# One rotation of four PSUM pairs after the tail, conversions one step a block, and the last stage's rows gathered four blocks ahead of their mixing

## The chip, the cores and the metric

The kernel runs on one core of a Trainium2 chip. The metric is device time in microseconds (us), from start to end of one execution of the program. The engines named below are PE (TensorE, matrix products), DVE (VectorE), ACT (ScalarE), POOL (GpSimd) and SP (SyncE, which here only issues DMAs). Each works through its own list of instructions in order and waits on semaphores for the others.

## The reference

Three layers follow each other on 2304 tokens of width 512, all in float32:

```
scores = q @ k.T / 8                              # 4 x 8 heads, 576 x 576
attn   = softmax(scores where >= rowmax - tau)    # the others are masked
x      = attn @ v                                 # 2304 x 512

y      = logits of x @ w_gate, plus noise * log1p(exp(x @ w_noise))
for e in 8 experts:                               # each token goes to its top 2
    out[mask] += weight * (relu(x[mask] @ w1[e]) @ w2[e])

a, b   = out @ m_w1, out @ m_w2                   # 512 -> 1024 each
h      = (a * b) @ w3
result = h @ w_out                                # 1024 -> 512
```

The weights of the last layer reach the chip as float64 bit patterns; the kernel turns them into float32 itself ("conversion"). Since w3 and w_out are applied one behind the other, the kernel multiplies them once into one matrix.

## The kernel before, in words

The order of the instructions on each engine is the order in which the Python code issues them; nothing reorders it. Up to about 397 us (attention, routing, and the "tail", a hand-written list of steps that starts expert 0) the change moves nothing but the names of PSUM pools.

**Experts (397 to 899 us of the trace).** Each expert has 640 token slots in five row blocks. *Phase 1* makes the hidden layer in eight blocks f = 0 to 7 (`phase1_steps`, L767): 12 passes over 256 and 384 columns into a tile S of two PSUM banks. ACT takes the high half hh out of S (L778), DVE the low half hl (L780). S has two buffers, so block f may start when DVE is through with block f-2. *Phase 2* has five blocks j (`phase2_steps`, L799 to L801): 24 products of 512 columns into a tile o of one bank, which is scaled into y and stored to the DRAM array ydr. Beside that run, for the next expert: `x_gather` (POOL, an indirect DMA, L685) and, two blocks later, the sum of squares on ACT (`x_sq`, L694); the scaling (L700); the transposes into a tile t of one bank, with two buffers (`x_trans`, PE L714, then ACT xth L717 and DVE xtl L718); weight loads (SP), their largest square (L730), a scale per weight matrix (`w_scale`, with a product on PE in `col_all`, L151) and the split of each weight chunk into two halves (`w_split`, ACT L749, DVE L750).

**Conversions.** `conv_step` advances every live conversion by one of five stages and starts a new one every second time. Stage 0 is a load (SP), stage 2 one POOL instruction (cr, L1018) and three of DVE (L1019 to L1021), stage 3 two of POOL (L1026, L1029) around one of DVE (L1027), stage 4 a store (SP) and for the last 16 of the 40 a maximum on DVE (L1035). From expert 1 on, conv_step runs 4 times in phase 1 (f = 0, 5, 6, 7) and 9 times in phase 2 (once for j = 0, twice for j = 1 to 4); f = 1 to 4 are those in which w_split runs.

**Last stage (from 855 us).** First w3 @ w_out in eight products (`w_prod`); the first is cut in two halves around a branch that handles overflowing experts and is not taken here. Then the 18 row blocks of 128 tokens in six groups of three. For a group g, `ab(g, f)`, f = 0 to 7, makes eight blocks of a * b (PE L1339 into S, ACT, DVE, ACT, and POOL for the remainder cl); at f = 2, `outp` multiplies the group before (L1359 to L1361 into o, three times). For the next group, `y_gather` fetches each token's two expert rows from ydr (POOL, L1297), `y_mix` weighs and adds them (ACT L1304, DVE L1305, ACT L1306, three short ones on DVE, POOL L1308), `y_trans` transposes them (PE L1319). In a group, gather, mix and transpose of its row block j stand at f = j, j + 1 and j + 4 of the group before: the mix is issued one block behind its gather. While group 0 runs, the splits of the weights (`wab_split`, four; `wf_split`, six of eight) also stand in its blocks.

**PSUM.** Eight banks of 2 KB per partition. From the tail's end on: S has two buffers of two banks, t two of one, o two of one.

Of the kernel before, what the change touches and what calls it, by code (L numbers as in the profile page):

```python
# [9 lines left out]
F32 = mybir.dt.float32  # L10
F32R = mybir.dt.float32r
F16 = mybir.dt.float16
# [7 lines left out]
PSUM = bass.MemoryType.PSUM  # L20
DRAM = bass.MemoryType.DRAM

B, H, S, D = 4, 8, 576, 64
HP = H // 2
NT = B * S // 128
# [42 lines left out]
def moe_kernel(ctx, tc, qT, kT, v, tau, wgn, noise, w1, w2, m1, m2, w3T, wo, out):  # L68
# [7 lines left out]
    px = ExitStack()  # L76
    px_pool = px.enter_context(tc.tile_pool(name="px", bufs=1, space=PSUM))
    late = {}

    def ps_s():  # L80
        return psum.tile([128, 2, 512], F32, name="S")

    def ps_t():
        return psum.tile([128, 512], F32, name="t", tag="ot")

    def ps_o():
        if late:
            return late["o"].tile([128, 512], F32, name="o")
        return psum.tile([128, 512], F32, name="o", tag="ot")
# [839 lines left out]
    late["o"] = ctx.enter_context(tc.tile_pool(name="po", bufs=2, space=PSUM))  # L929
# [60 lines left out]
    SP.dma_start(table, IDX)  # L990
    cctx = ExitStack()
# [102 lines left out]
    for e in range(E):  # L1094
        more = e + 1 < E
        for f in range(8):
            if e > 0:
                if f == 1:
                    next(sc2)
                    y_scale(e, 0, NBLK)  # L1100
                if 1 <= f < 5:
                    w_split(e, 2, f - 1)
            phase1(e, f, (1,) if e == 0 else (0, 1))
            if e > 0 and f == 0:
                next(sc2)
            if more:
                if f < NBLK:
                    x_gather(e + 1, f)
                if f < 4:
                    w_load(e + 1, 1, f)  # L1110
                if 2 <= f < 2 + NBLK:
                    x_sq(e + 1, f - 2)
                if f >= 4:
                    w_sq(e + 1, 1, f - 4)
                if f == 7:
                    x_pow2(0, NBLK)
            elif f == 5:
                WOT[0] = raw_load(wA, wod[0].rearrange("p a n -> p (a n)"))
            if e > 0 and not 1 <= f < 5:
                conv_step()  # L1120
# [16 lines left out]
        for j in js:  # L1137
# [22 lines left out]
            if more:  # L1160
                if at == 0:
                    for c in range(4 if e == 0 else 2):
                        w_load(e + 1, 2, c)
                if at == 1:
                    if e > 0:
                        next(sc1)
                        for i in range(3, NBLK):
                            x_scale(e + 1, i)
                        for c in range(2, 4):
                            w_load(e + 1, 2, c)  # L1170
                if j >= 3:
                    for c in range(2):
                        w_sq(e + 1, 2, 2 * (j - 3) + c)
                if j == NBLK - 1:
                    sc2 = w_scale(e + 1, 2)
                    next(sc2)
                for _ in range(2 if e > 0 and j else 1):
                    conv_step()
# [6 lines left out]
    def w_prod(m, k0=0, k1=8):  # L1185
# [12 lines left out]
        t = wf_.tile([128, DM], F32, name="wf")  # L1198
# [17 lines left out]
    def wf_split(m):  # L1216
        t = WF[m]
        h, l = (hp_.tile([128, CAP], F16, name=n)[:, :DM] for n in ("hh", "hl"))
# [16 lines left out]
    w_prod(0, 0, 4)  # L1235
# [58 lines left out]
    def y_gather(i):  # L1294
        t = xe.tile([128, 2, DM], F32, name=("xth", "xtl")[i % 2])
# [73 lines left out]
    NGR = NT // GN  # L1369
    for m in range(8):  # L1370
# [10 lines left out]
        w_prod(m, 0 if m else 4)  # L1381
# [11 lines left out]
    for g in range(NGR):  # L1393
        for f in range(8):
# [4 lines left out]
            if g + 1 < NGR:  # L1399
                i = (g + 1) * GN  # L1400
                if 1 <= f < 1 + GN:
                    y_mix(i + f - 1)
                if f < GN:
                    y_gather(i + f)
# [8 lines left out]
            if g + 1 < NGR:  # L1413
                if 4 <= f < 4 + GN:
                    y_trans(i + f - 4)
# [44 lines left out]
```

## Time and profile before

| | |
|---|---|
| time, median of 3 runs | 1212.92 us (1211.73 to 1216.4) |
| profiled execution | 1211.47 us, of which the span from first to last instruction is 1209.1 us |
| PE busy | 1072.8 us (89% of the span) |
| DVE, ACT, POOL busy | 687.1 (57%), 632.5 (52%), 605.1 us (50%) |
| DMA | 179.62 MB, mean 149 GB/s |
| mean granted clock of PE | 0.973 |

A share of busy time is a mean over stages that differ. The chain that ended last runs through PE for most of the last stage. A row of the views below gives times in us; "x" is a count; "<-" stands between a result and its inputs, or between a waiting instruction and what released it. The granted clock is 1.00 at 2.4 GHz and 0.50 at 1.2 GHz; a value between them is a mean over a stretch.

### The profile page before, as it was taken

What the parts mean: (1) busy time and instruction counts of PE and PEld (TensorE: products, weight loads), DVE (VectorE), ACT (ScalarE), POOL (GpSimd) and SP (SyncE); (2) the same over time, 40 slices, a digit from 0 to 9 for tenths busy, and PEclk for the clock granted to TensorE, in tenths of its full rate; (3) what the DMA queues carried; (4) which work ended last, traced back from release to release, by engine and by line L of the source; (5) the groups of instructions that cost most, each with busy time, mean ns of one, the idle gap of its engine ahead of it and who ended that gap; (6) DMA issues with size and microseconds to landing.
All of it is one profiled execution on the core that took longest, in us unless ns stands there. A gap on an engine that the chain in (4) does not pass through costs nothing. (4 is left out here: it accounts for less than half of the span.)

```text
span 1209.1 us, 19702 instructions
## 1 busy us (share of the span) xinstructions
PE 1072.8 (89%) x7424; PEld 704.8 (58%) x7425; DVE 687.1 (57%) x1398; ACT 632.5 (52%) x1213; POOL 605.1 (50%) x585
## 2 busy tenths in 40 slices
PE   6888888776789799998989898989997999999998
PEld 4667666555578664645555555555774455555654
DVE  6887777788674277676676767574354321222211
ACT  6888889775543574654646464553244332322311
POOL 5888888775532056656575748450204322323211
PEclk9999999998889999999999998999998999999999
DMA  6999999966723456577775756533621112111000
GB/s 165 210 211 217 214 212 229 208 153 135 144 88 107 129 196 207 200 260 263 226 244 177 232 173 211 165 115 114 225 90 53 46 34 62 36 61 53 27 27 26
DMA packets 236193, 179.62 MB, mean 149 GB/s; under 512 B 169792, under 2 KB 192576, under 8 KB 236096
## 3 DMA queue, kind: packets, MB, share of 16 engines
q1 hardware_dynamic: 229856, 158.12, 49.7%
q0 software_dynamic: 6080, 19.93, 5.3%
q8 instruction: 59, 0.97, 0.3%
q10 hardware_dynamic: 160, 0.30, 0.1%
q14 instruction: 38, 0.31, 0.1%
HBM read 99.72 MB, written 37.30 MB: 113 GB/s over the span
## 5 line engine op out<-in xcount | busy, mean ns | idle before, releaser
L260 PE MATMUL S<-K,Q 128*128 128x288 f32 x576 | 181.8, 441 | 46.7 <-DVE p L282 41.7
L767 PE MATMUL S<-xth,w 128*128 128x256 f16 (+3 forms) x1024 | 197.2, 307 | 21.7 <-DVE hl L780 19.7
L1339 PE MATMUL S<-x2h,w 128*128 128x384 f16 x768 | 192.9, 329 | 11.0 <-DVE a__10489 L1343 7.2
L308 POOL TENSOR_TENSOR p<-p,p 128x512 f16<-128x512 f32 x140 | 159.1, 1163 | 53.0 <-ACT p L299 52.9
L767 PEld LDWEIGHTS <-w 128*128 128x128 f16 x1344 | 133.5, 99 | 83.1 <-issue 32.2
L1339 PEld LDWEIGHTS <-w 128*128 128x128 f16 x1152 | 113.5, 99 | 87.8 <-issue 16.0
L260 PEld LDWEIGHTS S<-K,Q 128*128 128x128 f32 x576 | 103.0, 199 | 74.4 <-issue 23.6
L282 DVE SCALAR_TENSOR_TENSOR p<-S,th,p 128x576 f32<-128x576 f32 x144 | 116.6, 810 | 47.9 <-ACT th L274 47.8
L271 ACT ACTIVATE p<-S,mn 128x576 f32<-128x576 f32 x144 | 105.8, 734 | 58.8 <-DVE mn L265 53.9
L1339 PE MATMUL S<-x2l,w 128*128 128x384 f16 x384 | 126.3, 329 | 0.5 <-DVE x2l L1323 0.5
L799 PE MATMUL o<-w,hh 128*128 128x512 f16 (+1 forms) x320 | 124.5, 389 | 1.0 <-ACT hh L778 1.0
L801 PE MATMUL o<-w,hl 128*128 128x512 f16 (+1 forms) x320 | 123.8, 387 | 0.0
L767 PE MATMUL S<-xtl,w 128*128 128x256 f16 (+3 forms) x512 | 121.0, 307 | 3.1 <-DVE xtl L718 3.0
L800 PE MATMUL o<-w,hh 128*128 128x512 f16 (+1 forms) x320 | 123.6, 386 | 0.0
L265 DVE TENSOR_REDUCE mn<-S 128x1 f32<-128x576 f32 x144 | 108.4, 752 | 16.6 <-PE S L260 16.2
L1018 POOL TENSOR_SCALAR cr<-s 128x512 uint32<-128x512 uint32 x40 | 82.5, 2064 | 65.7 <-DMA s<-in_wo 52.1
L749 ACT ACTIVATE w<-w,WS 128x1024 f16<-128x1024 f32 x56 | 63.2, 1143 | 58.9 <-DVE WS L139 58.9
L1029 POOL TENSOR_TENSOR ck<-ck,ct 128x512 f32<-128x512 f32 x40 | 53.4, 1334 | 77.7 <-DVE ct L1027 59.5
L780 DVE SCALAR_TENSOR_TENSOR hl<-S,hh 128x256 f16<-128x256 f32 (+3 forms) x128 | 57.3, 485 | 61.3 <-ACT hh L778 60.9
L339 PE MATMUL o<-vh,pT 128*128 128x64 f16 (+1 forms) x720 | 85.0, 199 | 5.0 <-DMA pT<-p 3.3
L750 DVE SCALAR_TENSOR_TENSOR w<-w,WS 128x1024 f16<-128x1024 f32 x56 | 73.7, 1328 | 23.9 <-ACT w L749 23.7
L299 ACT ACTIVATE p<-p 128x1536 f16<-128x1536 f32 (+1 forms) x104 | 86.4, 840 | 0.7 <-DMA pT<-p 0.3
(459 smaller groups left out, 2115.2 us busy)
## 6 DMA issues: line engine op xcount, KB each, us to landing
w<-in_w SPq DMA_DIRECT2D x64, 512.0 KB, 5.6
ydr<-y SPq DMA_DIRECT2D x40, 256.0 KB, 2.2
s<-in_w3T SPq DMA_DIRECT2D x16, 512.0 KB, 5.2
s<-in_m SPq DMA_DIRECT2D x16, 512.0 KB, 4.9
ydr<-zrow SPq DMA_DIRECT2D x26, 256.0 KB, 5.4
w<-in_v SPq DMA_DIRECT2D x16, 320.0 KB, 4.4
K<-in_kT SPq DMA_DIRECT2D x16, 288.0 KB, 3.9
Q<-in_qT SPq DMA_DIRECT2D x30, 144.0 KB, 3.4
```

The costliest lines, as they stand in the source:

```text
L260: PE.matmul(St[u][:, j, :288], qb[:, c0:c0 + 128], kt[:, j * 288:(j + 1) * 288], start=True, stop=True)
L265: DVE.tensor_reduce(MN[u], St[u][:, :, :288], axis=AX.XY, op=OP.max, negate=True)
L271: ACT.activation(Pt[g][:, i, :].rearrange("p (a n) -> p a n", a=2), St[u][:, :, :288], AF.Exp, bias=MN[u])
L282: DVE.scalar_tensor_tensor(p, St.pop(3 * g + i)[:, :, :288], TH.pop(3 * g + i), p, op0=OP.is_ge, op1=OP.mult, accum_out=RS[rk][:, rc:rc + 1])
L299: ACT.activation(P16[g][:, us, h], Pt[g][:, us, c], AF.Copy)
L308: eng.tensor_tensor(p[:, u, l], Pt[g][:, u, c], p[:, u, h], op=OP.subtract)
L339: PE.matmul(o, hi, vh[:, hs, c, :], start=(c == 0), stop=False)
L767: PE.matmul(S_[:, z, :x_.shape[2]], w_[:, f * 128:(f + 1) * 128], x_[:, d, :], start=(d == 0 and a == 0), stop=(d == 3 and a == 2))
L799: PE.matmul(py, h, wh, start=(f == 0), stop=False)
L800: PE.matmul(py, h, wl, start=False, stop=False)
L801: PE.matmul(py, l, wh, start=False, stop=(f == 7))
L1339: PE.matmul(S_[:, s_, :n], w_[:, d, s_, :], x_[:, d, :], start=(d == 0 and a == 0), stop=(d == 3 and a == 2))
```

## The change

After the tail, every PSUM tile (S, t and o alike) takes the next of four pairs of banks, in turn; a t or o uses one bank of its pair. conv_step runs once in each block: 8 times in phase 1 and 5 times in phase 2. The scale of the second weight matrix moves from the last block of phase 2 into blocks 0 to 2 of the next phase 1, and w_split one block later, to f = 2 to 5. In the last stage, a gather stands four blocks ahead of its mix, in three buffers of its own; the mix moves one block later, to f = j + 2, and the transpose stays at f = j + 4. The first w_prod stands whole ahead of the branch. Two tiles get other storage.

```diff
     const = ctx.enter_context(tc.tile_pool(name="const", bufs=1))
     psum = ctx.enter_context(tc.tile_pool(name="psum", bufs=2, space=PSUM))
 
-    px = ExitStack()
+
+    pt_ctx, px = ExitStack(), ExitStack()
+    pot = pt_ctx.enter_context(tc.tile_pool(name="pot", bufs=2, space=PSUM))
     px_pool = px.enter_context(tc.tile_pool(name="px", bufs=1, space=PSUM))
-    late = {}
+    late, deep, turn = {}, [], [0]
 
     def ps_s():
-        return psum.tile([128, 2, 512], F32, name="S")
+        turn[0] += 1
+        pool = deep[turn[0] % 2] if deep else psum
+        return pool.tile([128, 2, 512], F32, name="S")
 
     def ps_t():
-        return psum.tile([128, 512], F32, name="t", tag="ot")
+        if deep:
+            return ps_s()[:, 0]
+        return pot.tile([128, 512], F32, name="t", tag="ot")
 
     def ps_o():
+        if deep:
+            return ps_s()[:, 0]
         if late:
             return late["o"].tile([128, 512], F32, name="o")
-        return psum.tile([128, 512], F32, name="o", tag="ot")
+        return pot.tile([128, 512], F32, name="o", tag="ot")
     dram = ctx.enter_context(tc.tile_pool(name="dram", bufs=1, space=DRAM))
     ctx.enter_context(tc.manual_schedule())
 
...
                 n_y += 1
     assert next(ahead, 0) == next(early2, 0) == 0 and not mq.q and n_g == n_y == NBLK
     SP.dma_start(table, IDX)
+    po_ctx.close()
+    pt_ctx.close()
+    deep += [psum, ctx.enter_context(tc.tile_pool(name="pd", bufs=2, space=PSUM))]
     cctx = ExitStack()
     cv = cctx.enter_context(tc.tile_pool(name="cv", bufs=2))
 
...
         more = e + 1 < E
         for f in range(8):
             if e > 0:
-                if f == 1:
+                if f == 2:
                     next(sc2)
                     y_scale(e, 0, NBLK)
-                if 1 <= f < 5:
-                    w_split(e, 2, f - 1)
+                if 2 <= f < 6:
+                    w_split(e, 2, f - 2)
             phase1(e, f, (1,) if e == 0 else (0, 1))
             if e > 0 and f == 0:
+                sc2 = w_scale(e, 2)
+                next(sc2)
+            if e > 0 and f == 1:
                 next(sc2)
             if more:
                 if f < NBLK:
...
                     x_pow2(0, NBLK)
             elif f == 5:
                 WOT[0] = raw_load(wA, wod[0].rearrange("p a n -> p (a n)"))
-            if e > 0 and not 1 <= f < 5:
+            if e > 0:
                 conv_step()
         if more:
             sc1 = w_scale(e + 1, 1)
...
                 if j >= 3:
                     for c in range(2):
                         w_sq(e + 1, 2, 2 * (j - 3) + c)
-                if j == NBLK - 1:
-                    sc2 = w_scale(e + 1, 2)
-                    next(sc2)
-                for _ in range(2 if e > 0 and j else 1):
-                    conv_step()
+                conv_step()
 
 
     mctx.close()
...
 
     sab = wab_scale()
     next(sab)
-    w_prod(0, 0, 4)
+    w_prod(0)
 
     with tc.tile_pool(name="ov", bufs=1) as ov:
         N = E + 1
...
     X2, X2T, CH, CL = {}, {}, {}, {}
 
     def y_gather(i):
-        t = xe.tile([128, 2, DM], F32, name=("xth", "xtl")[i % 2])
+        t = wf_.tile([128, 2, DM], F32, name="yg", bufs=3)
         for k in range(2):
             POOL.indirect_dma_start(out=t[:, k, :], out_offset=None, in_=ydr[:, :],
                                     in_offset=bass.IndirectOffsetOnAxis(ap=YL[:, k, i:i + 1], axis=0))
...
         out_rows(t, i)
 
     NGR = NT // GN
+
+
+    def y_step(k, ahead=False):
+        for i in range(GN, NT):
+            at = (i // GN - 1) * 8 + 2 + i % GN
+            if at - 4 == k:
+                y_gather(i)
+            if not ahead:
+                if at == k:
+                    y_mix(i)
+                if at + 2 == k:
+                    y_trans(i)
+
     for m in range(8):
         if 4 <= m + 2 < 8:
             w3_load(m + 2)
...
             y_mix(m - 2)
         if m < GN:
             y_gather(m)
-        w_prod(m, 0 if m else 4)
+        y_step(m - 8, ahead=True)
+        if m:
+            w_prod(m)
         if 4 <= m < 4 + GN:
             y_trans(m - 4)
         if m in (1, 2):
...
                 for j in range(GN):
                     outp(g - 1, j)
             ab(g, f)
-            if g + 1 < NGR:
-                i = (g + 1) * GN
-                if 1 <= f < 1 + GN:
-                    y_mix(i + f - 1)
-                if f < GN:
-                    y_gather(i + f)
             if g == 0 and f < 4:
                 wab_split(f + 4)
             if g == 0 and f < 3:
...
                 wf_split(f - 2)
             if g == 1 and f < 2:
                 wf_split(f + 6)
-            if g + 1 < NGR:
-                if 4 <= f < 4 + GN:
-                    y_trans(i + f - 4)
+            y_step(g * 8 + f)
     for j in range(GN):
         outp(NGR - 1, j)
 
```

What this moves on POOL, in phase 1 of expert 4 (xg is a gathered row block, cr and ck are conversion stages). Before:

```order
L685 DMA xg<-xdr,IDX 128x512
L1018 TENSOR_SCALAR cr<-s_7480 128x512
L685 DMA xg<-xdr,IDX 128x512 x4
L1026 TENSOR_SCALAR ck<-cm 128x512
L1029 TENSOR_TENSOR ck<-ck,ct 128x512
```

Now:

```order
L693 DMA xg<-xdr,IDX 128x512
L1030 TENSOR_SCALAR cr<-s_7440 128x512
L693 DMA xg<-xdr,IDX 128x512
L1038 TENSOR_SCALAR ck<-cm 128x512
L1041 TENSOR_TENSOR ck<-ck,ct 128x512
L693 DMA xg<-xdr,IDX 128x512
L1030 TENSOR_SCALAR cr<-s_7539 128x512
L693 DMA xg<-xdr,IDX 128x512
```

Four gathers stood behind one another; now each stands behind a conversion step, and every second of those steps waits for DVE's ct.

On DVE, blocks f = 2 to 4 of the same phase (w is the low half of a weight chunk, hl that of the hidden layer). Before:

```order
L750 SCALAR_TENSOR_TENSOR w<-w,WS 128x1024
L780 SCALAR_TENSOR_TENSOR hl<-S,hh 128x256
L780 SCALAR_TENSOR_TENSOR hl<-S,hh 128x384
L750 SCALAR_TENSOR_TENSOR w<-w,WS 128x1024
L780 SCALAR_TENSOR_TENSOR hl<-S,hh 128x256
```

Now:

```order
L758 SCALAR_TENSOR_TENSOR w<-w,WS 128x1024
L788 SCALAR_TENSOR_TENSOR hl<-S,hh 128x256
L788 SCALAR_TENSOR_TENSOR hl<-S,hh 128x384
L1047 TENSOR_REDUCE MS<-ck 128x1
L1031 TENSOR_SCALAR cm<-s_8190 128x512
L1032 TENSOR_SCALAR ct<-s_8190 128x512
L1033 SCALAR_TENSOR_TENSOR ct<-s_8190,ct 128x512
L758 SCALAR_TENSOR_TENSOR w<-w,WS 128x1024
```

A conversion step now stands between the evacuation of a block and the weight split of the next.

On POOL in the last stage, around the end of a group (xth, xtl and yg are gathered rows, cl a remainder of a * b, the other xg the scaled mix). Before:

```order
L1347 TENSOR_TENSOR cl<-a__11110,ch 128x384
L1297 DMA xtl<-ydr,YL 128x512 x2
L1347 TENSOR_TENSOR cl<-a__11145,ch 128x384
L1308 TENSOR_SCALAR xg<-xg,ZS 128x512
L1297 DMA xth<-ydr,YL 128x512 x2
L1347 TENSOR_TENSOR cl<-a__11276,ch 128x384
L1308 TENSOR_SCALAR xg<-xg,ZS 128x512
```

Now:

```order
L1309 DMA yg<-ydr,YL 128x512 x2
L1359 TENSOR_TENSOR cl<-a__11081,ch 128x384
L1309 DMA yg<-ydr,YL 128x512 x2
L1359 TENSOR_TENSOR cl<-a__11116,ch 128x384
L1309 DMA yg<-ydr,YL 128x512 x2
L1359 TENSOR_TENSOR cl<-a__11151,ch 128x384
L1359 TENSOR_TENSOR cl<-a__11271,ch 128x384
L1320 TENSOR_SCALAR xg<-xg,ZS 128x512
```

The three gathers no longer stand behind a mix: all three are issued before the first of their mixes.

## Rows read from the trace of the kernel before

**Rows 1.** Waits of PE, 385 to 900 us: total, times, longest

```profile
PE S L767 <- DVE hl L780: 18.9, 12, 4.0
PE t L714 <- DVE xtl L718: 13.6, 6, 3.0
PE S L767 <- DVE xtl L718: 3.0, 4, 1.0
PE t L714 <- DVE c L600: 2.6, 1, 2.6
```

**Rows 2.** Waits of PE, 899 to 1209 us: total, times, longest

```profile
PE S L1339 <- DVE a__10489 L1343: 7.2, 1, 7.2
PE o L1359 <- ACT hh L1219: 1.8, 1, 1.8
...
PE S L1339 <- DVE a__12157 L1343: 0.7, 1, 0.7
```

**Rows 3.** Stretches: length, busy per engine, granted clock, DMA share, GB/s

```profile
397.00:546.00 149.00, 133.07 (x747) 81.49 (x746) 94.97 (x183) 85.64 (x155) 74.14 (x67) 0.95 0.59 199
...
609.00:641.00 32.00, 27.85 (x193) 19.18 (x191) 20.56 (x37) 18.87 (x39) 21.74 (x15) 0.95 0.63 218
641.00:732.00 91.00, 83.47 (x477) 47.13 (x476) 64.35 (x112) 49.53 (x87) 58.33 (x36) 1.00 0.62 198
732.00:763.00 31.00, 26.60 (x172) 17.80 (x171) 20.46 (x36) 16.23 (x33) 19.00 (x13) 0.89 0.56 179
...
928.50:935.00 6.50, 6.45 (x24) 3.25 (x24) 3.07 (x6) 3.99 (x7) 1.60 (x2) 0.59 0.16 42
```

**Rows 4.** Chain that ended last, in group 0: start, us, what

```profile
908.67 3.54 DMA xtl<-ydr,YL
...
912.31 0.76 DVE xg L1305
...
921.69 0.76 DVE xg L1305
...
923.96 0.69 POOL xg L1308
...
940.27 3.91 PE S L1339 x24
```

**Rows 5.** Timeline in phase 1 of expert 4, DVE then ACT: start, us

```profile
635.72 0.89 DVE L780 SCALAR_TENSOR_TENSOR hl<-S,hh 128x256 f16<-128x256 f32 x2 [2.37 <-ACT hh L778]
...
638.98 0.89 DVE L780 SCALAR_TENSOR_TENSOR hl<-S,hh 128x256 f16<-128x256 f32 x2 [1.77 <-ACT hh L778]
...
638.18 0.77 ACT L778 ACTIVATE hh<-S 128x256 f16<-128x256 f32 x2 [0.70 <-PE S L767]
```

**Rows 6.** Groups, 600 to 800 us: count, busy us, mean ns, idle before

```profile
L1018 POOL TENSOR_SCALAR cr<-s 128x512 uint32<-128x512 uint32 x22 | 45.2, 2056 | 12.0 <-DMA s<-in_m 5.6 <-DMA s<-in_w3T 4.9
L1026 POOL TENSOR_SCALAR ck<-cm 128x512 f32<-128x512 int32 x22 | 37.0, 1684 | 11.5 <-DVE cm L1019 10.3
L750 DVE SCALAR_TENSOR_TENSOR w<-w,WS 128x1024 f16<-128x1024 f32 x26 | 34.4, 1332 | 10.6 <-ACT w L749 10.6
...
L1029 POOL TENSOR_TENSOR ck<-ck,ct 128x512 f32<-128x512 f32 x21 | 28.0, 1335 | 45.4 <-DVE ct L1027 41.1 <-DVE WS L735 3.8
L685 POOL DMA_INDIRECT xg<-xdr,IDX x15 | 21.0, 1402 | 4.0 <-issue 2.3 <-ACT hh L778 1.2 <-ACT w L749 0.3
L1021 DVE SCALAR_TENSOR_TENSOR ct<-s,ct 128x512 int32<-128x512 int32 x22 | 18.2, 828 | 0.8
L1027 DVE SCALAR_TENSOR_TENSOR ct<-cr,ct 128x512 int32<-128x512 int32 x21 | 15.5, 740 | 1.5 <-POOL cr L1018 1.0
L1020 DVE TENSOR_SCALAR ct<-s 128x512 int32<-128x512 int32 x22 | 14.3, 648 | 0.0
...
L1019 DVE TENSOR_SCALAR cm<-s 128x512 int32<-128x512 int32 x21 | 10.1, 480 | 4.5 <-DMA s<-in_w3T 3.1 <-DMA s<-in_m 1.4
```

**Rows 7.** Tile xg, 600 to 800 us: its gathers, from issue to landing

```profile
DMA to landing us min/median/max: 4.4/6.6/7.9
```

More of the change, by code (lines that the diff above doesn't have):

```diff
@@ L928, in moe_kernel @@
     px.close()
-    late["o"] = ctx.enter_context(tc.tile_pool(name="po", bufs=2, space=PSUM))
+    po_ctx = ExitStack()
+    late["o"] = po_ctx.enter_context(tc.tile_pool(name="po", bufs=2, space=PSUM))
     xe = ctx.enter_context(tc.tile_pool(name="xe", bufs=1))
@@ L1197, in w_prod @@
             return
-        t = wf_.tile([128, DM], F32, name="wf")
+        t = hp_.tile([128, CAP], F32, name="hh")[:, :DM]
         ACT.activation(t, po, AF.Copy)
@@ L1217, in wf_split @@
         t = WF[m]
-        h, l = (hp_.tile([128, CAP], F16, name=n)[:, :DM] for n in ("hh", "hl"))
+        hl = hp_.tile([128, 2 * CAP], F16, name="hl")
+        h, l = hl[:, :DM], hl[:, DM:2 * DM]
         ACT.activation(h, t, AF.Copy, scale=FS[:, 10:11])
```

## The prediction

> **What bounds the kernel now.** I read the waits of PE first, since PE is busy 89% of the span and the chain that ended last runs through it. In the expert stage PE waits 18.9 us in phase 1 for the low half hl of the block two before, which frees one of the two S buffers, 13.6 us for xtl, which frees one of the two t buffers, 2.6 us for the counts' tile c, which holds a t buffer too, and 3.0 us for the last xtl of an expert [rows 1]: 38.1 us. All four name DVE. The reader is to see that these are waits for a buffer or a late DVE, none of them for a load. In the last stage PE waits 7.2 us once for a product a, 1.8 us for a split weight, and four times 0.6 to 0.7 us (2.5 us) for a product [rows 2]: 11.5 us. The chain shows why: DVE's mixing step waits for a gather of 3.54 us, and the next gather stands behind that mix on POOL, so mixes follow each other every 9.4 us (912.31 to 921.69) while a block of PE takes 3.91 us [rows 4].
>
> The second view is the granted clock, because a wait costs again when PE comes back at 1.2 GHz. It is 0.95 over 149 us, 0.95 over 32 us and 0.89 over 31 us [rows 3]. Half-rate work costs the share missing from 1.00: 7.5 + 1.6 + 3.4 = 12.5 us. Some of the half-rate time lies inside the waits themselves, so I take 11 us. In the last stage 0.59 over 6.5 us, PE busy throughout, is 2.7 us [rows 3]. So 38.1 + 11 + 11.5 + 2.7 = 63.3 us could go.
>
> **Four pairs in phase 1.** PE takes 3.26 us a block (hl starts at 635.72 and 638.98), ACT's hh 0.77, DVE's hl 0.89 us [rows 5]. With two buffers PE runs on while hl comes at most 3.26 - 1.66 = 1.6 us later than it could; with four turns 3 x 3.26 - 1.66 = 8.1 us, and 4.9 us for the two blocks that have the scale's tile between them and their predecessor. Whether the 18.9 us go is thus a question of how far DVE falls behind.
>
> **Conversions.** An expert has 13 steps before and after, with the same loads, stores and zero rows on SP's queue, so nothing is added. Two steps cost DVE 0.48 + 0.65 + 0.83 + 0.74 = 2.70 us, 1.35 us each [rows 6]. Phase 2 loses four steps, 5.4 us of DVE, just where PE waits for xtl. The last t of an expert also waits no more for the t two before, but for an o. So 13.6 + 2.6 go, and of the 3.0 all but 0.4 in expert 0, whose steps stay as they were: there ACT is late on a weight load. Phase 1 gains the four steps. In f = 2 to 5 two blocks of DVE hold two hl (1.78), two splits (2.66) and a pair of steps (2.70), 7.14 us against 6.52 of PE. Four blocks leave DVE 1.2 us behind, and with the splits' waits for ACT some 2 to 4 us. That is below 4.9 and 8.1, so I take all 18.9 as gone, hidden under three blocks of PE.
>
> What is late next is the start of phase 2. Its first product reads the last hl only at its 22nd of 24 passes; from the columns (12,288 against 7,680 in 3.26 us) it lasts 5.2 us, so that is 4.5 us in, against 1.66 us plus a lag of 2 to 4: up to 1.2 us late. The added wait is on POOL: a gather now stands behind a conversion step, whose second POOL instruction waits for DVE's ct, and behind it stand the later gathers; ACT waits for them in the sum of squares, and behind that stands hh. Two blocks of POOL hold 2.06 + 1.68 + 1.34 + 2 x 1.40 = 7.88 us [rows 6] against 6.52, so the fifth gather is some 3 us late; its 1.40 us of issue and 6.6 us to landing [rows 7] already exceed the two blocks by which the squares lag. The squares feed the scale of the first transpose in phase 2. From both sides: 0 where blocks 6 and 7 make it good, 3.7 us where they don't. Blocks 6 and 7 have no split, so I take 1.6 us per expert, 9.6 us for six, and with 0.4 in expert 0 and 1 in expert 7, 11 us of new or remaining waits.
>
> **Scale and split of the second weight matrix, one block later.** Its reduction, its product on PE and its splits keep their number. The splits now end at f = 5, and phase 2 needs them after f = 7: two blocks of PE cover them, so nothing. Without that cover one split, 1.33 us [rows 6], would be late per expert.
>
> **Last stage.** The gathers are issued four blocks, 15.6 us, ahead against 3.54 us of transfer, so DVE no longer waits there and the 11.5 + 2.7 us lose their cause. On POOL a gather's two issues (nearest row: 1.40 us each [rows 6]) now stand among the remainders: 2.8 of 3.91 us, which leaves 1.1 us for a remainder, an instruction of about the 0.69 us of the scaling [rows 4]; nothing. What is late next is group 0: its blocks 2 to 4 each hold, besides product, copy and remainder, a weight split of 1024 columns (nearest row: 1.33 us), in two of them, one of half the size (0.7, estimate) and a mix that takes 2.27 us from DVE's sum to POOL's scaling (921.69 to 923.96) [rows 4, 6]. ACT and DVE alternate in it, so these add up to 4.3 us, against 3.91 us a block, before the product's own steps. The transpose stands only two blocks behind its mix. I take 5 us of PE waiting, between 0 and 9 (three blocks by 3 us). In later groups three products o, each 5.2 us, stand in front of the mixes, and no split.
>
> The four pairs don't help there: between S of two blocks of f = 4 to 7 stands a t, so S waits for the S two before, as now. The first w_prod stands whole ahead of the branch; ACT's copy and DVE's maximum move with it, and the next w_prod, 5.2 us of PE, covers them: nothing, at worst 2 us. Storage of the two tiles: nothing, either way.
>
> **The sum.** Against the profiled execution, 1211.5 us: waits gone 38.1 + 11.5, clock 11 + 2.7, waits left or new 11 + 5. That is 63.3 - 16 = 47.3 us, hence 1164.2. The median of the runs is 1.4 us above that execution: 1165.6, say 1165 us.
>
> **A rule against it.** The clock stayed at 1.00 over 91 us in which PE was idle for 7.5 us, in pieces [rows 3], so I expect the short waits that are left to cost no clock. The Trainium skill ("TensorE: Matmul & The Clock Gate", "A second HAM failure mode: psum-queue depth-cycling") tells of a kernel that cycled through PSUM banks and whose clock fell again and again through small pauses between groups of matmuls. By that rule the clock would not come back; the 91 us speak against it.
>
> **Rivals.**
> - *Everything is covered.* No new wait: 1211.5 - 38.1 - 12.5 - 11.5 - 2.7 = 1146.7, with 1.4 us 1148. For it: 8.1 us of slack. Against: POOL's 7.88 in 6.52 us. Chance 0.14.
> - *The clock doesn't come back* although the waits do: 1165 + 13.7 = 1179. Chance 0.06.
> - *DVE and POOL hold each other up.* The two short DVE instructions L1020 and L1019 have the same form and take 0.65 and 0.48 us, so something stretches them [rows 6]. If in each of the eight blocks of phase 1 one DVE instruction waits for half a POOL instruction (0.84 us), DVE is 6.7 us further behind, some 6 us of it beyond the slack: six experts, 36 us, 1201. The Trainium skill ("SBUF — State Buffer", "Who interferes with whom") says that a DVE instruction with two SBUF inputs and a GpSimd one that reads SBUF exclude each other; the 0.65 against 0.48 is in line with it. Against: the means that I used hold such cases. Chance 0.13.
> - *The turns don't deepen phase 1*, because t, o and the scale's tile take them: 18.9 us and about 8 us of clock stay, 1192. Against: one such tile in eight blocks. Chance 0.04.
> - *Slower: the gather loop of phase 1.* From a step's ct: POOL's product 1.34, gather 1.40, landing 6.6, then ACT's hh 0.77, hl 0.89 and the next ct 0.74: 11.7 us for three blocks that take 9.8 [rows 5 to 7]. Two rounds in a phase cost 4 us, six experts 24. That alone gives 1189; each microsecond more of landing adds 12 us, so it decides from a landing of 8.6 us, and at 10.6 the kernel takes 1237. For it: ACT's squares stand behind the gathers. Against: 7.9 us is the longest landing here. Chance 0.04; another 0.03 for a landing near 8.6, no change.
>
> **Chances and range.** My forecast has 0.56, with its own range of 1153 to 1176 (new waits between 4 and 27 us). I tell half a per cent, 6 us, from no change. Faster: the first five cases, 0.93, less 0.01 for the port rival's worst, 0.92; same 0.04; slower 0.04. For 8 in 10 the range leaves out a part of the covered case and the two slowest ones: 1146 to 1192.
>
> **What would show it.** Right: PE's waits for hl in phase 1 below 3 us; no wait of a t for xtl; no DMA of gathered rows in the last stage's chain; the clock at 1.00 in the expert stage. New waits then name the first transposes of phase 2 and hl at its start, and in group 0 the scaled rows. Wrong: ACT idle before the sum of squares for more than 4 us an expert, or DVE busy without a gap through phase 1 while PE waits for S.

## The result and the profile after

The changed kernel takes 1154.97 us (median of 4 runs, 1153.46 to 1156.6) against 1213.56 us (1211.73 to 1216.4): a ratio of 0.9515, with a 95% interval of 0.9492 to 0.9539. The profiled span (of the slowest of the four runs after) went from 1209.1 to 1154.5 us, 54.6 us. Line numbers shift between kernels: L767 before, L775 after and L776 in the experiments are the same statement. The forecast of 1165 us had the direction and the places right and was 10 us too slow.

The waits of PE after, 385 to 855 us, total, times, longest; they answer to [rows 1]:

```profile
PE S L722 <- ACT xg L708: 3.9, 6, 0.9
PE S L775 <- ACT xth L725: 1.7, 1, 1.7
PE S L722 <- ACT y L815: 1.3, 1, 1.3
...
PE S L775 <- DVE xtl L726: 0.4, 1, 0.4
```

The waits for hl (18.9 us) and the waits of t for xtl (13.6 us) are gone. New are six short waits of the first transposes of a phase 2 for their scaled rows, 3.9 us in all, and one in which a t must take a pair whose product o ACT has not yet moved into y.

The same view of the last two stages, 855 to 1160 us; it answers to [rows 2]:

```profile
PE S L1331 <- POOL xg L1320: 3.6, 3, 1.5
PE S L1351 <- DVE x2l L1335: 0.7, 1, 0.7
```

The 7.2 us for a product a and the 2.5 us for later products are gone. What is left lies in group 0 and names POOL's scaling of the mix. The stretches after (length, busy time and count of PE, weight loads, DVE, ACT, POOL, then granted clock, DMA share, GB/s) are expert 0's second half, experts 1, 2 and part of 3, the rest of the experts, group 0 and the later groups; they answer to [rows 3]:

```profile
397.90:423.00 25.10, 22.45 (x95) 17.21 (x94) 7.59 (x16) 13.38 (x24) 0.00 (x0) 0.86 0.38 126
423.00:546.00 123.00, 119.35 (x732) 72.64 (x732) 92.89 (x184) 76.04 (x141) 87.09 (x74) 0.99 0.73 244
546.00:810.00 264.00, 261.98 (x1592) 156.76 (x1589) 191.88 (x336) 151.41 (x276) 153.24 (x97) 1.00 0.65 210
...
857.60:895.90 38.30, 33.67 (x207) 20.00 (x205) 19.75 (x40) 20.50 (x37) 11.39 (x13) 1.00 0.05 14
895.90:1154.50 258.60, 254.48 (x1439) 141.68 (x1438) 56.83 (x129) 72.72 (x144) 68.78 (x77) 1.00 0.14 43
```

The clock is 0.99 to 1.00 from expert 1 on; in expert 0's second half it is lower than before (0.86 against 0.93). Experts 1 to 7, with practically the same number of matmuls, can now be set side by side: the first row is of the kernel before, the second of after.

```profile
421.10:852.40 431.30, 392.98 (x2319) 231.59 (x2319) 287.85 (x519) 229.21 (x417) 242.19 (x170) 0.98 0.60 198
```

```profile
423.00:810.00 387.00, 381.33 (x2321) 229.40 (x2320) 284.77 (x519) 227.45 (x417) 240.33 (x170) 1.00 0.67 221
```

They lost 44.3 us. PE's idle time fell from 38.3 to 5.7 us (length less busy), which is 32.6; the other 11.7 is busy time, the same matmuls at a higher clock. DVE did the same work, 287.85 and 284.77 us, so practically nothing became cheaper on it; the work lies elsewhere in time. The rest of the 54.6: 0.8 in expert 0's second half (25.9 to 25.1), 12.7 in the last stage (309.6 to 296.9), less 0.5 in the stage of products before it and 2.7 in the tail, whose instructions did not change.

In the last stage's chain no gather is left, and from 895.96 on it is matmuls; the first piece of these (start, us, what) answers to [rows 4]:

```profile
895.96 7.80 PE S L1351 x47
```

### The profile page after: what moved, and what is told of

Read it like the earlier page. It is cut to its first block, busy times and chain, and to the rows that moved or that the text cites. A ratio compares the mean times of both kernels' runs of the same rounds, so it can differ in the third digit from the quotient of the medians.

```text
span 1154.5 us, 19682 instructions
## 1 busy us (share of the span) xinstructions
PE 1060.1 (92%) x7424; PEld 703.5 (61%) x7425; DVE 685.2 (59%) x1398; ACT 630.7 (55%) x1213; POOL 601.6 (52%) x585
## 5 line engine op out<-in xcount | busy, mean ns | idle before, releaser
L775 PE MATMUL S<-xth,w 128*128 128x256 f16 (+3 forms) x1024 | 191.9, 304 | 3.4 <-ACT xth L725 1.7
L775 PEld LDWEIGHTS <-w 128*128 128x128 f16 x1344 | 132.0, 98 | 55.2 <-issue 3.7
L775 PE MATMUL S<-xtl,w 128*128 128x256 f16 (+3 forms) x512 | 118.5, 303 | 0.4 <-DVE xtl L726 0.4
L807 PE MATMUL S<-w,hh 128*128 128x512 f16 (+1 forms) x304 | 116.5, 383 | 0.9 <-ACT hh L786 0.9
L1030 POOL TENSOR_SCALAR cr<-s 128x512 uint32<-128x512 uint32 x40 | 87.9, 2197 | 55.6 <-DMA s<-in_wo 45.7
L809 PE MATMUL S<-w,hl 128*128 128x512 f16 (+1 forms) x304 | 116.3, 382 | 0.0
L808 PE MATMUL S<-w,hh 128*128 128x512 f16 (+1 forms) x304 | 116.2, 382 | 0.0
L348 PE MATMUL o<-vl,pT 128*128 128x64 f16 (+1 forms) x720 | 85.4, 199 | 0.0
L758 DVE SCALAR_TENSOR_TENSOR w<-w,WS 128x1024 f16<-128x1024 f32 x56 | 78.1, 1407 | 10.1 <-ACT w L757 9.7
```

The lines of the kernel that those rows point to most:

```text
L775: PE.matmul(S_[:, z, :x_.shape[2]], w_[:, f * 128:(f + 1) * 128], x_[:, d, :], start=(d == 0 and a == 0), stop=(d == 3 and a == 2))
L807: PE.matmul(py, h, wh, start=(f == 0), stop=False)
L808: PE.matmul(py, h, wl, start=False, stop=False)
L809: PE.matmul(py, l, wh, start=False, stop=(f == 7))
L1030: POOL.tensor_scalar(self.r, self.L, 4026531584.0, 268435456.0, op0=OP.min, op1=OP.add)
```

## The experiments

Theory A: all three parts are needed; the turns let PE pass a late DVE and bring the 18.9 us of hl, the conversions the 13.6 us of xtl, the gathers the last stage. Rival B: DVE's backlog alone was the cause, so that spreading the conversions makes the turns nearly idle. Except where said, each kernel is the one after with the shown edit; kernels shown together ran on one chip with the kernel before. Distances to the kernel after are taken across chips, unless said; the kernel before took 1211.67 to 1214.81 us on them.

**The turns undone.**

```diff
-    po_ctx.close()
-    pt_ctx.close()
-    deep += [psum, ctx.enter_context(tc.tile_pool(name="pd", bufs=2, space=PSUM))]
+    ctx.push(pt_ctx.__exit__)
+    ctx.push(po_ctx.__exit__)
...
-    w_prod(0)
+    w_prod(0, 0, 4)
...
-        if m:
-            w_prod(m)
+        w_prod(m, 0 if m else 4)
```

> The changed kernel, but with the PSUM pools of the kernel before (S two pairs, t and o two banks each; the first w_prod in two halves again). Theory A (four turns carry the gain of the expert stage, the even conversions alone cannot): two S buffers allow DVE a lag of 1.6 us, and a conversion step beside a weight split in f = 2 to 5 makes 2 to 4 us, so PE waits for hl again, 4 to 6 us an expert, more than before; the waits of t for xtl fall below 6 us in all. 1185 to 1200 us. Rival B (it is the spreading of the conversions that removes the waits): no wait for hl above 1 us, 1155 to 1162 us.

Measured: 1161.71 us (1159.2 to 1163.35), ratio 0.9567 [0.9528, 0.9607]; before 1214.81. The longest of PE's waits:

```profile
PE S L776 <- DVE hl L789: 9.1, 9, 1.9
```

The time is rival B's, at the upper end of its range; its sign, no wait for hl above 1 us, is not met (1.9). Half of the 18.9 us for hl goes by the spread conversions alone. The turns are worth about 7 us here, and this is not clear of the noise: the intervals of this ratio and of the kernel after (0.9492 to 0.9539) overlap.

**The old conversions.**

```diff
-                if f == 2:
+                if f == 1:
...
-                if 2 <= f < 6:
-                    w_split(e, 2, f - 2)
+                if 1 <= f < 5:
+                    w_split(e, 2, f - 1)
...
-            if e > 0:
+            if e > 0 and not 1 <= f < 5:
                 conv_step()
...
-                conv_step()
+                for _ in range(2 if e > 0 and j else 1):
+                    conv_step()
```

(with the scale of the second matrix back in the last block of phase 2)

> The changed kernel, but with conversion steps, the scale and the splits of the second weight matrix where they were (4 steps in phase 1, 9 in phase 2). Theory A: no wait for hl in phase 1; in phase 2 DVE is over-full where two steps stand in a block, so the first pass of the next expert waits for the last xtl, some 2 to 3 us an expert: 1165 to 1178 us. Rival C (the four turns alone do it, where the conversions stand doesn't matter): 1153 to 1159 us.

Measured: 1173.41 us (1172.5 to 1174.84), ratio 0.966 [0.9624, 0.9697], 18 us above the kernel after: theory A's range, and rival C is out. Its waits, and the stretch 530 to 546 us of this kernel:

```profile
PE S L808 <- DVE xtl L727: 12.0, 6, 3.0
PE S L776 <- DVE xtl L727: 5.3, 5, 1.7
```

```profile
530.00:546.00 16.00, 11.98 (x69) 6.69 (x67) 15.76 (x28) 8.97 (x15) 11.85 (x7) 1.00 0.73 232
```

No wait names hl: four pairs do carry PE over a late hl. But xtl, with the same pairs, is awaited for 17.3 us, and DVE is busy 15.76 of 16 us. The two rows are not the same kind of wait. In the 5.3 us (L776) xtl is data: the first pass of the next expert reads it, and no number of buffers helps there. In the 12.0 us (L808, once in each of six experts) a product of phase 2 that does not read xtl waits for a pair: four turns earlier a t took it, and DVE has not yet read that t. At 535.93, for instance, PE goes on when DVE has made the xtl of a t that was transposed at 525.48. So four pairs, too, are too few for a DVE that is some 10 us behind. This edit puts three things back together, conversion steps, scale and splits; which of them fills DVE was not tried apart.

**The old gathers in the last stage.**

```diff
-        t = wf_.tile([128, 2, DM], F32, name="yg", bufs=3)
+        t = xe.tile([128, 2, DM], F32, name=("xth", "xtl")[i % 2])
...
-            y_step(g * 8 + f)
+            if g + 1 < NGR:
+                i = (g + 1) * GN
+                if 1 <= f < 1 + GN:
+                    y_mix(i + f - 1)
+                if f < GN:
+                    y_gather(i + f)
...
```

> The changed kernel, but with gather, mix and transpose of the last stage where they were (gather one block ahead of the mix, two buffers). Theory A: mixes follow each other every 9.4 us again; the deeper S hides at most one or two blocks of that, so group 0 waits 8 to 14 us in S and in the transposes, and the later groups little: 1163 to 1170 us. Rival D (the deeper S hides the gathers, the move ahead is worth nothing): 1153 to 1158 us.

Measured: 1166.67 us (1164.16 to 1174.17), ratio 0.9618 [0.9565, 0.9672], 11.7 us above the kernel after. Its longest wait:

```profile
PE S L1343 <- DVE FS L1229: 4.8, 1, 4.8
```

The time is theory A's, and rival D is out. Waits that end on DVE are back in group 0, this one and one of 2.5 us for a product a, and 11.7 us is close to what the last stage gained (12.7).

**One part alone: the turns, then the conversions.** (The other parts as in the kernel before.)

> The kernel before with the four turns alone; conversions and gathers as before. Theory A: e2 and e3 add up, so as far above the changed kernel as both together: 1175 to 1190 us; the waits for hl in phase 1 are gone, those for xtl at the start of the next expert and in group 0 stay. Rival B: within 5 us of the kernel before, 1208 to 1218 us.

> The kernel before with one conversion step a block (and the scale and splits of the second weight matrix one block later), without the turns and with the old gathers. After e1 to e4 theory A is changed to A2: DVE's backlog at the end of phase 2 is the cause of both kinds of waits; spreading the conversions takes the backlog away, the turns only give it room. Then the conversions alone bring about 53 us less the 11 us of the gathers: 1170 to 1177 us, and PE waits for hl about 9 us in all. Rival E (the turns and the conversions need each other): 1190 to 1205 us.

Measured: the turns alone 1183.82 us (1181.16 to 1187.35), ratio 0.9741 [0.9702, 0.978]; the conversions alone, on the next chip (before 1214.6), 1175.23 us (1174.15 to 1177.01), 0.9682 [0.9619, 0.9744]. Waits of the first, then of the second:

```profile
PE S L808 <- DVE xtl L727: 10.5, 6, 2.6
PE S L776 <- DVE xtl L727: 7.4, 7, 1.7
```

```profile
PE S L776 <- DVE hl L789: 9.8, 8, 2.6
```

For the turns alone theory A's range held and rival B's did not; the conversions alone came out as A2 had it, hl included. Alone they bring 31 and 39 us, with the gathers changed as well 41 (1173.41) and 53 (1161.71), and all three some 59. If turns and conversions added up, it would be 31 + 39 + 12 = 82. Each does much of the other's work: they are two remedies for one backlog, and the turns are nearly idle only where the conversions are already spread.

**A late DVE, with the turns and without.** Six extra operations on a scratch tile, ahead of block 0 in experts 1 to 7:

```diff
+            if e > 0 and f == 0:
+                for _ in range(6):
+                    DVE.scalar_tensor_tensor(lagt, lagt, 1.0, lagt, op0=OP.mult, op1=OP.add)
             phase1(e, f, (1,) if e == 0 else (0, 1))
```

> The changed kernel with six more DVE instructions of 128x512 (about 0.7 us each, 4.1 us) on a scratch tile ahead of block 0 of phase 1 of experts 1 to 7; nothing else changes. A2: with four turns phase 1 bears a lag of 4.9 to 8.1 us, so no wait for hl inside phase 1; what is left of the lag shows at the first transposes of phase 2, 0 to 1.5 us an expert: 0 to 10 us above the changed kernel. Rival F (DVE is full, so every microsecond put on it costs one): 7 x 4.1 = 29 us more.

> The same six DVE instructions in the kernel of e1 (no turns). A2: two S buffers bear 1.6 us, so PE waits 4.1 - 1.6 = 2.5 us for hl of block 0 and a little more in the blocks with splits, 2.5 to 4 us in each of seven experts: 17 to 30 us above e1. Rival G (the depth of S doesn't matter once the conversions are spread): the same as e6, 0 to 10 us above e1.

Measured: 1161.0 us (1157.38 to 1162.02), 0.9567 [0.9506, 0.9628], with the turns, 6 us above the kernel after; 1165.37 us (1162.76 to 1166.43), 0.9593 [0.9531, 0.9655], without, 3.7 above the kernel that it extends where 17 to 30 were expected. The timeline without turns in expert 4, DVE and then PE's first matmuls of block 0, shows why the pair told nothing:

```profile
596.55 5.58 DVE L1124 SCALAR_TENSOR_TENSOR lagt<-lagt 128x512 f32<-128x512 f32 x6
602.06 0.88 DVE L789 SCALAR_TENSOR_TENSOR hl<-S,hh 128x256 f16<-128x256 f32 x2
```

```profile
597.06 0.43 PE L776 MATMUL S<-xth,w 128*128 128x256 f16 x2
```

PE began block 0 only at 597.06. With 3.26 us for the block and 0.77 for hh, hl could start at 601.1 at the earliest: the extra work fell largely into a gap in which DVE has nothing to do (4.47 us in the kernel after, shown further down), and hl came 1 us late instead of 5.

**The gathers of the next expert earlier.**

```diff
-                if f < NBLK:
-                    x_gather(e + 1, f)
+                for i in ((0, 1), (2, 3), (4,))[f] if f < 3 else ():
+                    x_gather(e + 1, i)
```

> The changed kernel with the five gathers of the next expert's rows two in block 0, two in block 1 and one in block 2 of phase 1, ahead of those blocks' conversion steps. A2 with the prediction's chain (a gather behind a conversion step makes the sum of squares late, and that the first transpose): ACT's 16.2 us of waiting for gathered rows fall below 5 us and PE's waits of the first transpose for the scaled rows, 3.9 us, below 1.5 us: 1151 to 1154 us. Rival H (the first transpose is late because ACT and DVE are behind anyway): ACT's wait goes but PE's 3.9 us stay, 1154 to 1156 us.

Measured: 1152.66 us (1151.29 to 1154.51), 0.9492 [0.9431, 0.9553]: inside A2's range, but not to be told from the kernel after. ACT's waits for the landing and for the scale, 423 to 810 us, in the kernel after, and then the one that is left here:

```profile
ACT sqj L702 <- DMA xg<-xdr,IDX: 16.2, 8, 3.5
ACT xg L708 <- DVE XS L147: 7.0, 6, 2.9
```

```profile
ACT xg L709 <- DVE XS L148: 17.3, 6, 4.2
```

The wait for the landing is gone, and that for the scale grew from 7.0 to 17.3 us; PE's wait at the first transposes only fell from 3.9 to 3.2 us. So A2's chain is wrong at this place: in the kernel after, the landing was not what PE waited for.

**A late DVE again, where DVE is full.** The same six operations, but ahead of block 3 (f == 3 in the diff above), and with them a kernel of three edits and the kernel after once more.

> The kernel after, with six extra VectorE operations of 128x512 on a scratch tile ahead of the hl of block 3 of phase 1 in experts 1 to 7 (5.5 us an expert by the e6 trace, where six took 5.59 us). There VectorE works back to back in the kernel after, so hl of blocks 3 to 7 comes some 5 us later, unlike in e6 and e7, where the six ran while TensorE filled the first block. Theory A2 (the turns give VectorE room: slack 4.9 to 8.1 us against 1.6): hl may be some 7 us late before TensorE waits, 0 to 2.5 us an expert, so 0 to 17 us above the kernel after: 1155 to 1172. Rival G (the turns give no room): as much above the kernel after as e10 is above e1, within 7 us. Rival H (VectorE has idle time enough): 0 to 5 us, and e10 too.

> The same six operations in the kernel without the turns (that of e1, 1161.7). Theory A2: with two pairs TensorE waits from 1.6 us of lateness on, so 4 to 5.5 us in each of seven experts, 28 to 38 us above e1: 1188 to 1202, with 25 us or more of waits for hl in phase 1 above the 9.1 of e1. Rival G: as much above e1 as e9 is above the kernel after. Rival H: 0 to 5 us above e1.

Measured, on a chip where before takes 1211.67 us: with the turns 1189.67 us (1185.53 to 1190.24), 0.9813 [0.978, 0.9846]; without 1201.05 us (1198.72 to 1201.77), 0.991 [0.9879, 0.9941]. That is 37.0 above the kernel after on this chip (1152.7), where A2 had 0 to 17, and 39.3 above the kernel without turns, which ran on another chip (1161.71): by the totals, rival G's result, though A2's 1188 to 1202 held without turns. The waits, with the turns first:

```profile
PE S L723 <- ACT xg L709: 9.5, 7, 2.5
PE S L808 <- ACT hh L787: 7.8, 5, 3.2
...
PE S L776 <- DVE hl L789: 3.5, 2, 3.0
PE S L810 <- DVE hl L789: 3.3, 7, 0.8
```

```profile
PE S L776 <- DVE hl L789: 38.1, 10, 5.9
```

The mechanism of A2 is in them all the same. Without turns the lateness is paid in phase 1 (38.1 us for hl); with them PE runs through phase 1 in all but two cases (3.5 us) and pays at the border to phase 2, in other names. Three rows of experts 1 to 7 show the price: the late DVE with turns, then the kernel without turns (that of the first experiment), then the same with the late DVE:

```profile
421.39:843.20 421.81, 396.12 (x2321) 233.05 (x2321) 313.34 (x561) 227.65 (x417) 245.60 (x170) 0.96 0.62 203
```

```profile
420.19:814.50 394.31, 382.54 (x2321) 229.73 (x2320) 284.53 (x519) 229.30 (x417) 242.30 (x170) 1.00 0.66 217
```

```profile
419.43:856.50 437.07, 397.12 (x2321) 235.54 (x2321) 314.04 (x561) 229.26 (x417) 244.91 (x170) 0.95 0.59 196
```

PE's idle time (length less busy) is 25.7 us with turns, 20 more than in the kernel after (5.7); without turns it is 40.0, 28 more than the 11.8 of the kernel that it extends. So the turns take about 8 of 28 us of the waiting. Both pay some 15 us more in busy time besides, at a clock of 0.96 and 0.95. Expert 4 with the turns: DVE's hl of blocks 0 and 3, PE at the border, ACT, POOL, and the stretch around the border:

```profile
613.74 0.89 DVE L789 SCALAR_TENSOR_TENSOR hl<-S,hh 128x256 f16<-128x256 f32 x2 [4.68 <-ACT hh L787]
...
629.88 0.88 DVE L789 SCALAR_TENSOR_TENSOR hl<-S,hh 128x256 f16<-128x256 f32 x2
```

```profile
635.67 0.38 PE L808 MATMUL S<-w,hh 128*128 128x512 f16 x1
...
641.33 0.39 PE L808 MATMUL S<-w,hh 128*128 128x512 f16 x1 [0.96 <-ACT hh L787]
...
642.17 0.39 PE L810 MATMUL S<-w,hl 128*128 128x512 f16 x1 [0.23 <-DVE hl L789]
643.90 1.11 PE L723 MATMUL S<-ident,xg 128*128 128x128 f32 x4 [1.34 <-ACT xg L709]
644.80 0.63 PE L808 MATMUL S<-w,hh 128*128 128x512 f16 x1
```

```profile
639.10 0.63 ACT L703 ACTIVATE sqj<-xg 128x512 bf16<-128x512 f32 x1 [5.72 <-DMA xg<-xdr,IDX]
...
640.91 0.74 ACT L787 ACTIVATE hh<-S 128x256 f16<-128x256 f32 x2
```

```profile
631.51 2.18 POOL L1046 TENSOR_TENSOR ck<-ck,ct 128x512 f32<-128x512 f32 x1 [3.38 <-DVE ct L1044]
633.84 1.05 POOL L694 DMA_INDIRECT xg<-xdr,IDX  x1 [0.15 <-issue]
```

```profile
636.00:660.00 24.00, 21.47 (x98) 10.10 (x96) 18.37 (x35) 13.55 (x22) 16.87 (x11) 0.93 0.69 222
```

PE reads the last hh and hl some 4.5 us into phase 2. Up to there nothing waits in this expert, although hl of block 3 was some 6 us late (629.88, against 613.74 and three blocks of 3.26 us, 623.5). Then three waits, 2.5 us, and matmuls of 0.63 in place of 0.38 us. ACT's hh stands behind a sum of squares that waited 5.72 us for a gather; the gather (issued at 633.84) stands on POOL behind the step that waited 3.38 us for the late DVE. This is the loop of gathers that the prediction had as its slower rival. That it, and not hl alone, makes hh late is read from these rows and was not tried apart.

**Three edits for the waits that are left.** The early gathers above; in expert 0 the last sums of squares in the last block; and the mix a block earlier:

```diff
-            at = (i // GN - 1) * 8 + 2 + i % GN
-            if at - 4 == k:
+            at = (i // GN - 1) * 8 + 1 + i % GN
+            if at - 3 == k:
...
-                if at + 2 == k:
+                if at + 3 == k:
...
-                if j >= 3:
-                    for c in range(2):
-                        w_sq(e + 1, 2, 2 * (j - 3) + c)
+                if j >= (3 if e else 4):
+                    for c in range(2) if e else range(4):
+                        w_sq(e + 1, 2, 2 * (j - 3) + c if e else c)
```

> The kernel after with three edits: the gathers of the next expert's rows in the blocks 0, 0, 1, 1, 2 of phase 1 (e8: 2 us), rows of the last stage mixed one block earlier and gathered three blocks ahead in place of four (aims at the 3.6 us that TensorE waits for POOL's mixing in group 0), and in expert 0 the four w_sq of the third matrix in the last block of phase 2 (aims at 1.7 and 0.4 us). Each works alone: 1155 less 2, 3 and 2 is 1147 to 1151. Rival (the waits move to the gather's landing, since three blocks in group 0 are some 16 us but VectorE and POOL lie closer): group 0 keeps its 3.6 us, and the time is 1151 to 1154.

> The kernel after, instruction for instruction, on the same chip as e9 to e11, to compare them with: 1153 to 1157.

Measured: 1152.12 us (1148.79 to 1155.1), 0.9513 [0.9484, 0.9542], against 1152.7 us (1150.82 to 1157.04), 0.9524 [0.9495, 0.9553]: no gain to be told. The time is the rival's, its reason is not. The first wait of the last stages with the edits:

```profile
PE S L1363 <- DVE a__10542 L1367: 3.1, 1, 3.1
```

The 3.6 us for POOL's scaling are gone, and 3.1 us for a product stand in their place. In expert 1 the 1.7 and 0.4 us are gone too, but 1.5 us for a scale (L160 for WS) and 1.3 us for hl are new. It looks as if DVE and ACT had more to do in these places than the blocks give them, so that a new order only changes which of their results is late; no run takes work out of group 0 to show it.

## Why the prediction was right, and where its sizes were off

- **Waits gone, 38.1 us in the experts.** All but 0.4 us went. But the text gave the 18.9 us of hl to the turns, and that was too much: with the turns undone PE waits 9.1 us for hl, and the whole kernel is some 7 us slower. The larger cause was the load on DVE in phase 2, with two conversion steps in a block; its backlog made xtl late, and since half of the wait for hl goes with it, it also ran on into phase 1. DVE's lag in phase 1 itself is small. Expert 4 in the kernel after, DVE, hl of blocks 0 and 5:

```profile
597.65 0.89 DVE L788 SCALAR_TENSOR_TENSOR hl<-S,hh 128x256 f16<-128x256 f32 x2 [4.47 <-ACT hh L786]
...
616.08 0.88 DVE L788 SCALAR_TENSOR_TENSOR hl<-S,hh 128x256 f16<-128x256 f32 x2
```

  The first comes as soon as hh is there. Five blocks of 3.26 us later is 613.95, so the other, the latest of the eight, is some 2.1 us late: within the 2 to 4 us of the text.
- **Slack of the turns, 4.9 to 8.1 us.** It holds only inside phase 1. At the border it is 4.5 - 1.66 = 2.8 us, from the text's own numbers, which it used for the next wait and not for the worth of the turns.
- **Clock, 11 us.** Experts 1 to 7 gave back 11.7 us of busy time, and expert 0 lost 0.8. Most waits that are left are short and cost no clock: over 264 us, with three of them of up to 0.9 us, it is 1.00. The longest, 1.7 and 0.4 us at the start of expert 1 (424.92 and 425.76), is followed by 3 us at half rate, which the text did not foresee:

```profile
427.00:430.00 3.00, 3.00 (x13) 1.66 (x11) 2.97 (x5) 2.62 (x5) 2.20 (x1) 0.50 0.63 175
```

  The kernel of which the Trainium skill tells ("TensorE: Matmul & The Clock Gate", "A second HAM failure mode: psum-queue depth-cycling") cycles through PSUM banks, and PE pauses between its groups of matmuls often enough for the clock to oscillate. Here four pairs in turn run at 1.00 over 264 us with 2.0 us of PE idle, so the pauses that the page names are missing, and this trace neither follows it nor speaks against it.
- **New or remaining waits, 11 us in the experts.** Mis-sized. The 1.6 us an expert were 0.6 (3.6 us in five waits of experts 1 to 7), and the 1 us of expert 7 did not come; that blocks 6 and 7 made good more of POOL's delay would fit, but is not shown, and the early gathers speak against the landing as its cause. The whole expert stage, experts 1 to 7 above and expert 0's second half before in this row,

```profile
395.20:421.10 25.90, 21.62 (x95) 16.53 (x94) 7.59 (x16) 13.07 (x24) 0.00 (x0) 0.93 0.38 122
```

  had 42.6 us of PE idle time before and has 8.3 after (5.7 and 2.6): 34.3 gone against the 27.1 of the sum. This is the 7 us by which the experts beat the forecast (45.1 against 38.1); busy time fell 10.8, as the text had it (11).
- **Last stage, 9.2 us.** Measured 12.7. The 5 us of group 0 were 4.3 of named waits (3.6 and 0.7), the larger part in the place and with the name foretold; the first of three:

```profile
879.33 0.66 PE L1331 MATMUL S<-ident,xg 128*128 128x128 f32 x4 [1.49 <-POOL xg L1320]
```

  The two stretches of the last stage before, group 0 and the rest:

```profile
899.50:937.90 38.40, 29.62 (x167) 17.12 (x166) 15.92 (x33) 16.61 (x29) 15.23 (x14) 0.87 0.15 42
937.90:1209.10 271.20, 261.87 (x1480) 145.57 (x1478) 60.02 (x135) 76.94 (x152) 72.21 (x79) 1.00 0.14 41
```

  Against the rows after, PE's busy time fell 3.3 us (2.7 in the sum), its idle time from 18.1 to 8.8 us, 2.9 more than the 6.5 of the sum, which had only the named waits.
- **Rivals.** DVE and POOL did not hold each other up by 6.7 us in a phase: the lag of 2.1 us bounds it. Its example does not fit what it cites for two SBUF inputs, since L1019 and L1020 read one tile each. The clock came back. The slower gather loop did not decide: ACT's 16.2 us for landings are 2.7 us in each of the six experts that gather for a next one, and taking them away (the early gathers) moved the time by nothing that can be told. The turns did deepen phase 1 (waits for hl of 3.5 us against 38.1 with the late DVE); only, with the conversions spread, they were hardly needed.
- **The sum.** 7.0 and 3.5 us more than forecast, less 0.5 and 2.7 in stages that were taken as unchanged, is 7.3: 54.6 against 47.3. Why the tail took 2.7 us longer stays open, but it is not the change: it ends at 395.2 us before and at 397.9 after, and at 395.0 in the kernel after on another chip, whose span was 1148.7.

## What to carry to other kernels

Where several waits name one engine, look first for the stretch in which that engine is full (15.76 of 16 us with the old conversions): undoing the move of its work costs 18 us here, undoing the deeper buffers about 7. A deeper rotation helps only against waits for a buffer, only for as many blocks as it has buffers, and only up to the next point at which the value itself is read; size it by that point. To test a slack, put the extra work where the engine has no idle time, and see in the trace that it came late.

## What the runs showed of the hardware

- Waits of 0.96, 0.23 and 1.34 us within 3 us were followed by half-rate matmuls and a clock of 0.93 over 24 us, and waits of 1.66 and 0.41 us by 3 us at 0.50; in the kernel after, three single waits of 0.3 to 0.9 us left the clock at 1.00. In seven experts with the late DVE the clock costs not much less than the waits: some 15 us of busy time against 20 us of idle time, by the rows of experts 1 to 7 above.
- The same split of 1024 columns takes 1.28 us at 604.38 and 1.70 us at 614.46, when a POOL conversion of 1.96 us has started at 614.44 (DVE, then POOL, in the kernel after):

```profile
604.38 1.28 DVE L758 SCALAR_TENSOR_TENSOR w<-w,WS 128x1024 f16<-128x1024 f32 x1 [0.53 <-ACT w L757]
...
614.46 1.70 DVE L758 SCALAR_TENSOR_TENSOR w<-w,WS 128x1024 f16<-128x1024 f32 x1
```

```profile
605.08 2.51 POOL L1030 TENSOR_SCALAR cr<-s 128x512 uint32<-128x512 uint32 x1
...
614.44 1.96 POOL L1030 TENSOR_SCALAR cr<-s 128x512 uint32<-128x512 uint32 x1
```

  At 605.08, with DVE's split already under way, it is POOL that takes longer, 2.51 us. That is in line with the Trainium skill ("SBUF — State Buffer", "Who interferes with whom"), by which a DVE instruction with two SBUF inputs, as this split is, contends with a GpSimd one that reads SBUF; two pairs of rows don't show more.
